# An attention and gated-convolution kernel: stages by a schedule table, and the carried state added on VectorE

## The chip, the cores and the metric

One core of one Trainium2 chip (trn2). Times are device microseconds (us) of one launch of the whole kernel. A run is called *slow* when it is over 1.5% above the fastest run of the same kernel in the same job; the ratios below use fast runs only. *Span* is the part of the time between the first and the last instruction in the trace, some 2 us less than the time. Engines: PE is TensorE, DVE is VectorE, ACT is ScalarE, POOL is GpSimd; SP issues the transfers.

## The reference, cut

```python
B, H, S, D = 4, 8, 768, 48
for t in range(S):                                    # linear attention with decay
    cur = einsum('bhd,bhe->bhde', u * k[:, :, t], v[:, :, t])
    y[:, :, t] = einsum('bhd,bhde->bhe', r[:, :, t], state + cur)
    state = w[..., None] * state + einsum('bhd,bhe->bhde', k[:, :, t], v[:, :, t])
x = y.transpose(0, 2, 1, 3).reshape(B, S, 384)
gate = sigmoid(causal_conv5(x, conv_w))               # one filter of 5 taps for each channel
out = (gate * (x @ w_val)) @ w_out
```

Both kernels work in chunks of 128 tokens and in units of two chunks: 12 units, three for each batch. Inside a chunk the recurrence is a masked attention; between chunks the state `z` is carried, decayed by `w` to the power 128. Four batches of six chunks need 20 state products, and 16 of them have an earlier state to add.

## The kernel before: what the change touches

The state of a chunk is four products into PSUM, and the carried state is added there by one more product, with the identity:

```python
def state(n, cl):
    # ... four products of ks and vb into kv_ps (cut)
    if c > 0:
        nc.tensor.matmul(
            out=kv_ps.rearrange("p n a d -> p (n a d)"),
            lhsT=ident,
            rhs=st["z"].rearrange("p n a d -> p (n a d)"),
            start=False, stop=True, skip_group_check=True,
        )

def decay(n, cl):
    # ... (cut)
    z = wk.tile([128, NP, 2, D], BF16, name="z", bufs=6)
    nc.vector.tensor_tensor(out=z, in0=st["kv_ps", n, cl], in1=wcm, op=ALU.mult)
```

The order of work is a plain loop, the same on every engine. It works on unit `i` and finishes unit `f = i - 1`; what prepares unit `i + 1` is called in between:

```python
w_bc = consts.tile([128, H, D], F32)
nc.sync.dma_start(out=w_bc, in_=w.partition_broadcast(128))
load_r(0)                       # r of a whole batch, then k and v of unit 0, k of unit 1
load_kv(0, "kv")
load_kv(1, "k")
# ... weights, more k and v (cut)
for i in range(N + 1):
    f = i - 1
    # ... loads of k and v of unit i + 3, of r of a later batch (cut)
    if ok(f):
        y_out(f)
    if ok(i + 1):
        cast_v(i + 1)
        scale_k(i + 1, nc.gpsimd)
    if ok(i):
        attn(i, 0); mask_at(i, 0); bonus(i); state(i, 0); decay(i, 0)
    # ... scaling of r, bonus_v(i), weight casts when i == 0 (cut)
    if ok(f):
        conv(f); value(f)
    if ok(i):
        attn(i, 1); mask_at(i, 1); state(i, 1); decay(i, 1)
    # ... transposes of r and k, prod(i + 1) (cut)
    if ok(f):
        project(f)
```

## Time and profile before

| | before |
|---|---|
| time, median of 3 runs | 119.07 us (118.67 to 119.47) |
| profiled run: span | 115.8 us |
| busy: PE, DVE, ACT, POOL | 86%, 58%, 63%, 57% of the span |
| first y products of unit 0, 3 and 11 start at | 22.95, 48.99, 105.69 us |

The first y products of a unit are the first thing that a round does on PE, so their start times cut the execution into a head (up to unit 3), steady rounds (units 3 to 11) and a tail. This is the busy time by stretch of the kernel before. Columns: stretch and its length in us, then busy us and instruction count of PE, weight loads, DVE, ACT and POOL, then granted PE clock, DMA share and GB/s.

```profile
22.95:48.99 26.04, 24.85 (x506) 18.37 (x505) 15.33 (x24) 18.70 (x31) 24.16 (x20) 0.87 0.99 239
48.99:105.69 56.70, 54.79 (x1272) 40.69 (x1272) 39.75 (x61) 38.35 (x70) 30.72 (x21) 1.00 0.66 161
105.69:115.80 10.11, 4.94 (x121) 3.48 (x120) 1.28 (x3) 3.47 (x8) 0.00 (x0) 0.95 0.23 80
```

The lines show three stages with different limits. In the head POOL is busy 24 of 26 us and the DMA share is 0.99. In the steady stage PE is busy 54.8 of 56.7 us and DVE only 39.8. In the tail no engine is full: it is one chain.

### The profile page before, as it was taken

What the parts mean: (1) busy time and instruction counts of PE and PEld (TensorE: products, weight loads), DVE (VectorE), ACT (ScalarE), POOL (GpSimd) and SP (SyncE); (2) the same over time, 40 slices, a digit from 0 to 9 for tenths busy, and PEclk for the clock granted to TensorE, in tenths of its full rate; (3) what the DMA queues carried; (4) which work ended last, traced back from release to release, by engine and by line L of the source; (5) the groups of instructions that cost most, each with busy time, mean ns of one, the idle gap of its engine ahead of it and who ended that gap; (6) DMA issues with size and microseconds to landing.
All of it is one profiled execution on the core that took longest, in us unless ns stands there. A gap on an engine that the chain in (4) does not pass through costs nothing.

```text
span 115.8 us, 4806 instructions
## 1 busy us (share of the span) xinstructions
PE 100.0 (86%) x2098; PEld 76.5 (66%) x2098; DVE 67.7 (58%) x120; ACT 73.0 (63%) x130; POOL 66.3 (57%) x62
## 2 busy tenths in 40 slices
PE   5999046889899999999979999999999999998840
PEld 5998043666667778768747786786777677775610
DVE  5425327926467737767665677774786877775120
ACT  4198375293388696886862958859667483935430
POOL 7942106799999949989549768190462805050000
PEclk9999975555999999999999999999999999999998
DMA  1899599999998998998999795994984030030303
GB/s 44 240 270 150 95 236 305 194 193 266 277 191 180 292 332 169 256 213 253 341 170 248 154 248 113 256 206 96 238 169 147 0 133 8 24 118 6 136 3 136
DMA packets 58677, 20.57 MB, mean 178 GB/s; under 512 B 50592, under 2 KB 58656, under 8 KB 58656
## 3 DMA queue, kind: packets, MB, share of 16 engines
q1 hardware_dynamic: 58432, 20.26, 73.2%
q8 instruction: 16, 0.26, 1.0%
q0 software_dynamic: 224, 0.01, 0.3%
q14 instruction: 5, 0.04, 0.1%
HBM read 15.54 MB, written 4.72 MB: 175 GB/s over the span
## 4 chain that ended last, share of the span: by engine, by line
PE 55%; ACT 10%; SPq 10%; POOL 10%; issue 6%; DMA 4%; DVE 1%; POOLq 0%; ACTq 0%; DVEq 0%
PE mm_ps L383 9%; PE mm_ps L456 9%; SPq L72 8%; PE mm_ps L426 6%; PE mm_ps L435 6%; PE mm_ps L475 6%; PE at_ps L317 5%; ACT kT L268 4%; DMA k_st<-in_k_dram 4%; PE tr_ps L238 3%; PE kv_ps L343 3%; POOL ks L245 3%; ACT o_sb L482 3%; ACT rT L239 3%; PE mm_ps L291 2%
## 5 line engine op out<-in xcount | busy, mean ns | idle before, releaser
L329 DVE TENSOR_TENSOR at<-at_ps,mask 128x1024 bf16<-128x1024 f32 x24 | 29.3, 1220 | 8.8 <-PE at_ps L317 8.8
L303 POOL TENSOR_TENSOR dv<-v_st,s_sb 128x768 bf16<-128x768 f32 x12 | 17.7, 1475 | 24.3 <-DVE s_sb L300 24.3
L245 POOL TENSOR_TENSOR ks<-k_st,dk 128x768 bf16<-128x768 f32 x11 | 20.0, 1815 | 5.5 <-DMA k_st<-in_k_dram 5.5
L463 DVE TENSOR_TENSOR hT<-mm_ps,gate 128x256 bf16<-128x256 f32 (+1 forms) x24 | 13.4, 558 | 15.3 <-PE mm_ps L456 15.3
L226 POOL TENSOR_TENSOR rs<-r_st,dr 128x576 bf16<-128x576 f32 x12 | 16.7, 1412 | 3.2 <-DMA r_st<-in_r_dram 3.1
L268 ACT COPY kT<-tr_ps 128x1024 bf16<-128x1024 bf16 x12 | 12.2, 1014 | 8.6 <-PE tr_ps L265 8.6
L239 ACT COPY rT<-tr_ps 128x768 bf16<-128x768 bf16 x15 | 11.9, 799 | 7.0 <-PE tr_ps L238 7.0
L475 PE MATMUL mm_ps<-wout,hT 128*128 128x384 bf16 x72 | 14.0, 327 | 1.2 <-DVE hT L463 1.2
L456 PE MATMUL mm_ps<-xT,wval 128*128 128x256 bf16 x108 | 13.8, 272 | 0.0
L254 ACT CAST vb<-v_st 128x768 bf16<-128x768 f32 x12 | 10.0, 836 | 5.2 <-DMA v_st<-in_v_dram 5.2
L482 ACT COPY o_sb<-mm_ps 128x384 f32<-128x384 f32 x24 | 10.7, 495 | 3.9 <-PE mm_ps L475 3.9
L279 DVE TENSOR_TENSOR pr<-tr_ps,rT 128x1024 bf16<-128x1024 bf16 x12 | 8.3, 692 | 7.9 <-ACT kT L268 7.6
L411 ACT CAST xT<-mm_ps 128x384 bf16<-128x384 f32 x24 | 11.8, 496 | 1.0 <-PE mm_ps L383 0.2
L317 PE MATMUL at_ps<-rT,kT 48*128 48x128 bf16 x192 | 10.4, 229 | 1.4 <-DVE rT L239 0.6
L456 PEld LDWEIGHTS <-wval 128*128 128x128 bf16 x108 | 10.6, 98 | 1.5
L368 DVE TENSOR_TENSOR z<-kv_ps,wcm 128x384 bf16<-128x384 f32 x20 | 11.0, 548 | 0.0
L265 PE MATMUL tr_ps<-ident,ks 128*128 128x128 bf16 x96 | 7.8, 227 | 3.3 <-DVE ks L245 3.1
L500 PE MATMUL mm_ps<-ident 128*128 128x128 bf16 x130 | 9.4, 248 | 1.4 <-POOL ident masks.py:199 1.4
L500 PEld LDWEIGHTS <-ident 128*128 128x128 bf16 x130 | 9.3, 114 | 1.4 <-POOL ident masks.py:199 1.4
L383 PE MATMUL mm_ps<-at,vb 128*32 128x128 bf16 x384 | 10.1, 227 | 0.0
L435 PE MATMUL mm_ps<-xT,cwd 128*128 128x256 bf16 x60 | 9.3, 286 | 0.9 <-issue 0.9
L444 ACT ACTIVATE gate<-mm_ps 128x512 bf16<-128x512 f32 x12 | 7.2, 597 | 4.6 <-PE mm_ps L435 4.6
(65 smaller groups left out, 150.5 us busy)
## 6 DMA issues: line engine op xcount, KB each, us to landing
k_st<-in_k_dram SPq DMA_DIRECT2D x24, 192.0 KB, 5.2
v_st<-in_v_dram SPq DMA_DIRECT2D x24, 192.0 KB, 5.2
out_dram<-o_sb SPq DMA_DIRECT2D x11, 384.0 KB, 4.0
r_st<-in_r_dram SPq DMA_DIRECT2D x6, 576.0 KB, 5.9
r_st<-in_r_dram SPq DMA_DIRECT2D x4, 288.0 KB, 5.6
wv_st<-in_moe_w_val_dram SPq DMA_DIRECT2D x1, 576.0 KB, 5.8
wo_st<-in_moe_w_out_dram SPq DMA_DIRECT2D x1, 384.0 KB, 5.4
out_dram<-o_sb SPq DMA_DIRECT2D x2, 192.0 KB, 1.9
```

Of the source, the lines that this page charges most:

```text
L226: eng.tensor_tensor(out=rs_t[p][:, :, :, 0:D].rearrange("p j a d -> p a j d"), in0=r_st[b][:, hs, :].rearrange("p a (j d) -> p a j d", d=D ...
L239: (nc.vector.tensor_copy if dve else nc.scalar.copy)(out=st["rT", b][:, p, :].rearrange("x (p j) -> x p j", j=J), in_=tr.rearrange("x j p ...
L245: eng.tensor_tensor(out=ks_t[n % 3][:, :, :, :, 0:D].rearrange("p c n a d -> p c (n a) d"), in0=k_st[n], in1=dk[:, None, :, :].to_broadcas ...
L268: nc.scalar.copy(out=st["kT", n].rearrange("x n (c i) -> x c n i", c=U), in_=tr)
L303: nc.gpsimd.tensor_tensor(out=dv_t[n % 2].rearrange("p c (h d) -> p (c h) d", d=D), in0=v_st[n].rearrange("p c h d -> p (c h) d"), in1=st[ ...
L317: nc.tensor.matmul(out=at_ps[:, par, p, :], lhsT=kT[rows, p, cs], rhs=rT[rows, p, cs], start=(p == 0), stop=(p == NP - 1), skip_group_chec ...
L329: nc.vector.tensor_tensor(out=st["at", n, cl].rearrange("p a n i -> p (a n) i"), in0=st["at_ps", n, cl].rearrange("p a n i -> p (a n) i"), ...
L383: nc.tensor.matmul(out=y_ps[32 * q : 32 * q + 32, T, :], lhsT=lt, rhs=rh, start=q not in first, stop=last, skip_group_check=True,)
L435: nc.tensor.matmul(out=g02[:, 1, :], lhsT=cwd2[:, t, :], rhs=xT[:, 2, t0 + t : t0 + t + W], start=False, stop=(t == KW - 1), skip_group_ch ...
L456: nc.tensor.matmul(out=v_ps[:, i, :], lhsT=wval[:, kt, ts.start + i, :], rhs=xT[:, kt, t0 : t0 + W], start=(kt == 0), stop=(kt == NT - 1),)
L475: nc.tensor.matmul(out=o_ps, lhsT=hT[:, i, cl * C : cl * C + C], rhs=wout[:, i, :], start=(i == 0), stop=(i == NT - 1),)
L500: nc.tensor.matmul(out=t_, lhsT=ident, rhs=ident, start=True, stop=True)
```

## The change

Its intent, as far as the code tells it: (1) the state is carried by a VectorE addition in place in PSUM, which takes the identity product off PE; (2) a text table, probably worked out with a model of the engines' queues, gives the order of some thirty stages, one item for each stage and half unit, so that what waits on one engine stands between items that don't; (3) loads come in the order of need, in pieces of one unit, and stores only when every load has been issued, with ten output buffers in place of three; (4) the tables that the head needs are smaller (decay of r with 2 columns in place of 6, convolution weights prepared on DVE); (5) masks, gates and gated products are split in halves for this, and the third convolution tile is computed as 64x64 blocks. Cut to its core (the numbers after a colon are unit offset and half; `~7` asks for that many warm-up products):

```diff
-        if c > 0:
-            nc.tensor.matmul(out=kv_ps..., lhsT=ident, rhs=st["z"]..., start=False, stop=True, ...)
+    def carry(n, cl):
+        kv_ps = st["kv_ps", n, cl]
+        nc.vector.tensor_tensor(out=kv_ps, in0=kv_ps, in1=st["zin", n, cl], op=ALU.add)
 ...
-    def load_r(b):                 # 288 or 576 KB of a batch, rows of 1152 B
+    def load_r(n):                 # 384 KB of a unit, rows of 384 B
 ...
-        at_ps = ps_at.tile([128, 2, NP, 128], F32, name="at_ps")
+        at_ps = [ps_at.tile([128, NP, 128], F32, name="at_ps") for par in range(2)]
 ...
-    for i in range(N + 1):
-        f = i - 1
-        ...
+    LOADS = """
+        r0 k0 r2 v0 r1 k1 k2 v1 Wv k3 Wo r3 v2 r4 v3 k4 v4 r5 k5 r6 k6 v5 k7 r7 v6 k8 v7 r8 k9 v8
+        r9 k10 v9 r10 k11 v10 r11 v11
+    """
+    HEAD = """ ... """             # units 0 to 3, item by item, with 30 warm-up products (cut)
+    STEP = """
+        Y:-1.0 YE:-1.0 Y:-1.1 A:0.1 YE:-1.1 M:0.3 A:0.0 RS:1.0 M:0.2 KS:1.0 M:0.0 CV:0.0 C:-1.0
+        S:0.0 M:0.1 RT:1.0 V:-1.0 SE:0.0 SG:-1.0 HT:-1.0 V:-1.1 KV:0.0 SG:-1.1 RE:1.0 HT:-1.1
+        ID:0.0 KT:1.0 KE:1.0 O:-1.1 O:-1.0 OE:-1.1 ZE:0.0 PR:1.0 KV:0.1 ID:0.1 OE:-1.0 ZE:0.1
+        DV:0.0
+    """
+    TAIL = """ ... """             # the end of unit 11 (cut)
+    run(HEAD, 0)
+    for i in range(HEAD_STEPS, N):
+        run(STEP, i)
+    run(TAIL, 0)
```

Here Y is the y products, A attention, M masks, C convolution, V value, O output projection, KV state products, ID the in-place addition, ZE decay, CV the cast of v; an E marks a copy out of PSUM.

## The prediction

> **What bounds the kernel now.** I read the page's busy sums and the 40 slices first, then the chain of work that ended last in order of time, then busy time by stretch, then the groups by form.
>
> ```profile
> PE 100.0 (86%) x2098; PEld 76.5 (66%) x2098; DVE 67.7 (58%) x120; ACT 73.0 (63%) x130; POOL 66.3 (57%) x62
> PE   5999046889899999999979999999999999998840
> ...
> PEclk9999975555999999999999999999999999999998
> DMA  1899599999998998998999795994984030030303
> ```
>
> TensorE (PE) is busy 86% of the span and nearly always after slice 10; the holes are in the first 30 us, where the granted clock is also halved. So there are two stages with different limits: a head up to about 35 us, and a steady part. The DMA row is full until about 80 us, so transfers are a near second bound.
>
> The chain in order of time shows the head:
>
> ```profile
> 13.09 4.30 DMA k_st<-in_k_dram
> ...
> 17.58 1.77 POOL ks L245
> ...
> 20.91 1.47 POOL dv L303
> 22.38 1.22 POOL cwd L198
> ```
>
> The chain runs through the queue that issues loads, the second k tile, then one GpSimd (POOL) instruction after another until 32 us. From 35 us it is PE. One steady round:
>
> ```profile
> 85.96 1.30 PE mm_ps L383 x80
> 87.26 0.33 PE at_ps L317 x8
> 87.59 0.28 PE mm_ps L291 x8
> 87.88 0.19 PE kv_ps L343 x4
> 88.07 0.67 PE mm_ps L426 x20
> 88.74 0.66 PE mm_ps L435 x5
> 89.40 0.98 PE mm_ps L456 x9
> ```
>
> There is no wait between these pieces. The rounds start (first y matmuls, L383) at 41.78 and 105.76 us, nine rounds apart: 63.98/9 = 7.1 us each. Busy time by stretch confirms it:
>
> ```profile
> 72.50:80.00 7.50, 7.49 (x174) 5.74 (x174) 5.03 (x9) 5.71 (x11) 3.25 (x2) 1.00 0.96 213
> 93.00:99.50 6.50, 6.44 (x146) 4.66 (x141) 4.86 (x8) 4.08 (x9) 1.48 (x1) 1.00 0.18 63
> ```
>
> Columns: stretch, length, then busy us of PE, weight loads, VectorE (DVE), ScalarE (ACT), POOL; clock, DMA share, GB/s. PE is full, DVE two thirds busy. Moving work from PE to DVE is the right direction.
>
> **What the Trainium skill says.** (1) "VectorE: DVE Perf Modes", section on the TRN2 errata: an fp32 tensor_tensor takes (N+151)/0.96 ns. The trace agrees, also with one operand in PSUM: 1224, 691 and 557 ns by the formula for N = 1024, 512, 384, against 1220, 692 and 548 measured.
>
> ```profile
> L329 DVE TENSOR_TENSOR at<-at_ps,mask 128x1024 bf16<-128x1024 f32 x24 | 29.3, 1220 | 8.8 <-PE at_ps L317 8.8
> L368 DVE TENSOR_TENSOR z<-kv_ps,wcm 128x384 bf16<-128x384 f32 x20 | 11.0, 548 | 0.0
> L463 DVE TENSOR_TENSOR hT<-mm_ps,gate 128x512 bf16<-128x512 f32 x12 | 8.3, 692 | 3.1 <-PE mm_ps L456 3.1
> L352 PE MATMUL kv_ps<-z,ident 128*128 128x384 bf16 x16 | 5.6, 350 | 0.0
> ```
>
> (2) "TensorE: Matmul & The Clock Gate", Part 1: the array falls to half clock after an idle window of about 3.4 us. The trace agrees: PE does nothing from 11.5 to 14.6 us and the clock is 0.50 from 16 to 30 us. (3) "PSUM — Partial Sum Buffer", on bank collisions: engines must be kept apart by bank, not by address. So with one state buffer the next chunk's state matmuls wait until both the new add and the decay have left the bank; the trace of before has only the decay there. (4) "DMA: Bandwidth & Descriptors", Specifications: below 512 B a transfer is not at line rate. The trace agrees: late stretches that only store rows of 1536 B move 63 GB/s at 0.18 share, 350 GB/s per full share, while the first k and v rows of 192 B move 134 to 164 GB/s at a full share (8 to 11 us).
>
> **The change part by part.**
>
> *PE, per unit of 256 tokens.* Removed: the identity product, 0.16 us in the chain, 16 in all, 4/3 per unit = 0.21 us. The third convolution tile, five 128x128 products (0.66 us), becomes 20 products of 64x64 on 128 columns. The existing 20 of that kind on 256 columns take 0.67 us, so half the columns is about 0.33 us: 0.33 saved. The value product has the same total of columns (9 x 256 = 6 x 256 + 6 x 128): unchanged. Transposes of r are the same 96, now 8 in each unit (0.45 us as for k) and no longer twelve in some rounds; those rounds lost another 0.3 us to ScalarE copies. Sum: 1.30 (y) + 0.66 (attention) + 0.28 (bonus) + 0.47 (state) + 0.67 + 0.33 (convolution) + 0.98 (value) + 0.90 (transposes) + 0.98 (project) = 6.57 us, against 7.1 now.
>
> *DVE, per unit.* Four masks of 512 at 0.69 = 2.77 (was 2 x 1.22 = 2.44); two gated products of 384 at 0.55 = 1.10 (was 0.69 + 0.43 = 1.12); decay 20 x 0.548/12 = 0.91; the new in-place add, 16 x about 0.55/12 = 0.73; bonus product 0.69; its copy 0.16. Sum 6.36 us, was 5.32. So DVE comes within 0.2 us of PE. The split masks buy something for this: the first half can begin when half the scores are there, in four banks in place of one pair.
>
> *ACT, per unit:* two y copies 0.99, k and r copies of 1024 elements 1.01 each, v cast 0.84, two sigmoids of 384 about 0.98, two output copies 0.99: 5.8 us. *POOL:* 1.82 + 1.48 + r scaling of 768 elements (1.41 for 576, so about 1.85): 5.15 us. Neither binds.
>
> *DMA.* Busy time now is 0.732 x 115.8 = 84.8 us per engine. Stores: 3072 rows of 1536 B at 70 ns (21.9 GB/s per engine, from the 63 GB/s at 0.18) / 16 = 13.4 us. That leaves 71 us of loads: r 4.72 MB and the weights and w 1.38 MB at the same rate per byte 13.5 and 3.9 us, so 54 us for the 24 k and v tiles of a unit, 2.25 each. r goes from 1152 B rows to 384 B rows, three times as many; if cost is per byte nothing is added, with a fixed cost per packet my estimate is up to 5 us. Loads: 71 to 76 us, about 6 per unit. Started at about 3 us, the last v lands at 74 to 79 us, and stores are held until every load is issued.
>
> *Head.* The order of loads is by need: one third of the r of a batch, then k, in place of the whole r of a batch and a broadcast w of 192 KB. The decay table has 2 columns in place of 6: two exponentials of 384 elements (0.6 us each) in place of twelve (4.3 us). Convolution weights leave POOL (3.8 us, L198 and L206 at 20 to 26 us) for DVE before the first data. Estimate: decay table ready at 5.7 us, first r scaled at 6.5, k landed at about 8, scaled and copied at about 10, first y products near 13.5 us (22.95 now). Then loads pace it: in the new order nine k and v tiles at 2.25, five of r at 1.4 (1.1 by bytes, 0.3 for the shorter rows) and 3.4 of weights stand up to k of unit 4, 31 us from a start at 3: it lands near 34 us, and the head table needs it at its end. PE work in the head: 3 units x 6.57 + 3.2 for what is prepared of units 3 and 4 = 22.9, plus warm-ups of 3, from 6.5 us: 32. So y of unit 3 starts at about 36 us. Now it starts at 49.3 (chain, the ACT o_sb piece before the y products at 49.82).
>
> *Sum.* Eight more rounds to y of unit 11. The pure PE pace is 6.57; with DVE at 6.36 on the other side of every hand-over I choose 6.8: 36 + 8 x 6.8 = 90.4. Tail: now 105.76 to 115.8 = 10.0 us; less 0.33 of convolution and about 0.7 by interleaving, 9. Span 99.4. The time was 119.07 for a span of 115.8, 3.3 more, though the profiled run itself was 117.56, only 1.8 more. I add 2: **101.5 us**, a gain of 15%: about 13 us from the head, 2 from the eight steady rounds, 1 from the tail.
>
> **The rivals.**
> *DVE becomes the bound.* For: 6.36 of 6.57, and the add lengthens the only serial chain (state matmuls, add, decay, next state matmuls in the same buffer) by 0.55 us twice per unit minus 0.16. Against: that chain is about 2.7 us of a 6.6 us round, and a table ordered in advance can fill around it. If so, rounds of 7.1 as now and no steady gain: 36 + 57 + 9 + 2 = 104, and 107 if the head suffers too.
> *DMA bounds it.* For: a full DMA row now and smaller r rows; a starved stretch such as 12 to 14 us now (share 0.40 and 0.23) may recur. Then v of unit 11 lands near 84, y at 87, end 96 to 98 of span if rounds keep pace, but held stores queue up behind: 100 to 106.
> *All goes nearly as the table plans:* rounds of 6.57 and y of unit 3 at 34: 34 + 52.6 + 8.5 + 2 = 97.
> *The head's gain is lost:* PE idles, the clock halves again, in-order queues wait on each other by a wrong model: first 36 us become 45, 110 us. The warm-up products (70 in all against 130 at once) speak against it.
>
> **Range and chances.** The rivals span 97 to 110; 95 to 108 should hold it. Slower by 2% would need the head gain lost and rounds of over 7.6 us at once. Faster 0.95, within 2% 0.03, slower 0.02.
>
> **What would show it.** Right: no matmul of z by the identity and 16 in-place adds near 0.55 us; DVE busy about 78 us and over 75% of the span; PE work down; y of unit 3 at 34 to 39 us; rounds of 6.6 to 7.0; clock full from about 10 us; stores only in the last third. Wrong: rounds of 7.1 or more with PE waiting for DVE; k or v loads as releasers after 40 us; half clock past 20 us; y of unit 0 after 17 us.

## The result, and the profile after

| | before | after |
|---|---|---|
| time, median of 4 runs | 119.08 us (118.67 to 119.47) | 105.53 us (104.37 to 108.75) |
| fast runs of after | | 104.37 and 105.05 us, spans 102.4 and 103.2 |
| slow runs of after | | 106.02 and 108.75 us; the latter is the profiled one, span 106.9 |
| ratio | | 0.8793 (95%: 0.8724 to 0.8863) |

The ratio is the mean time of one kernel's fast runs over that of the other's of the same rounds, so not quite the ratio of the medians. The change makes the kernel 12% faster in this job; measured again on chip 3 (a0 below) it is 9% (ratio 0.9103, 0.8948 to 0.9258), 106.47 against 117.04 us. The before of this job, 119.08 us, is the slowest of all jobs (fast means of 116.31 to 117.31 us in the others), so some 2 us of its gain may not be the change's. The profile of after is of a slow run, and this has to be kept apart from the rest: fast profiles come from two variants below that cost nothing measurable, the identity variant and the one with long warm-ups.

From the page of the kernel after: the sums, then rows of the 40 slices.

```profile
PE 92.6 (87%) x2263; PEld 74.2 (69%) x2263; DVE 76.4 (71%) x151; ACT 73.1 (68%) x120; POOL 64.4 (60%) x64
PE   4996775899999999899299999998999999999740
PEclk9999999557999999999859999999999999999999
DMA  0999989989988989889699989797979993310404
```

PE does 7.4 us less than before and DVE 8.7 us more. The hole in PE moved from the first quarter to one slice in the middle (a 2), with a dip of the clock behind it. The DMA row is full until about 88 us; its last full slices are the stores, which now wait for the loads.

From the groups of instructions by form (line, engine, operation, tiles, shapes, count; busy us and mean ns; idle before and what ended it):

```profile
L360 DVE TENSOR_TENSOR at<-at_ps,mask 128x512 bf16<-128x512 f32 x48 | 30.3, 682 | 7.4 <-PE at_ps L347 7.3
L387 DVE TENSOR_TENSOR kv_ps<-kv_ps,z 128x384 f32<-128x384 f32 x16 | 8.9, 557 | 1.0 <-PE kv_ps L375 0.9
L500 DVE TENSOR_TENSOR hT<-at_ps,gate 128x384 bf16<-128x384 f32 x24 | 12.8, 555 | 8.5 <-PE at_ps L487 8.2
```

The 16 in-place additions take 557 ns each and wait 1.0 us in all: they are there as forecast and are no bottleneck of their own. (48 masks of 682 ns would be 32.7 us; the row has 30.3 because two masks in a row overlap a little. The same holds for DVE as a whole: the 66 DVE instructions of the last six rounds below last 38 us one by one, and DVE is busy 35 us.)

Busy time by stretch of the kernel after, cut at the same events:

```profile
13.47:40.68 27.21, 24.69 (x571) 19.64 (x571) 20.30 (x38) 18.67 (x28) 20.32 (x15) 0.87 0.94 211
40.68:97.56 56.88, 52.95 (x1427) 42.62 (x1426) 45.82 (x87) 43.17 (x74) 35.03 (x21) 0.97 0.83 200
97.56:106.90 9.34, 4.58 (x158) 3.52 (x158) 1.05 (x2) 3.22 (x7) 0.00 (x0) 1.00 0.24 86
```

Set against before: unit 3 starts 8.31 us earlier, the eight steady rounds take 0.18 us *more* in this profile, and the tail 0.77 us less. 8.31 - 0.18 + 0.77 = 8.90 us, which is the difference of the two spans. The fast runs are another 3.7 to 4.5 us shorter. So two questions stand: where the gain of the head comes from and why it isn't larger; and what the steady rounds lost in the profiled run.

The six last rounds before the tail (units 5 to 11) leave out the hole in the middle. First the kernel before, then after, in the same columns:

```profile
64.33:105.69 41.36, 40.70 (x953) 30.32 (x953) 30.01 (x47) 27.94 (x52) 18.92 (x13) 1.00 0.54 130
```

```profile
57.80:97.56 39.76, 38.39 (x1071) 31.01 (x1070) 34.77 (x67) 31.47 (x55) 24.08 (x15) 1.00 0.78 202
```

A round went from 6.89 to 6.63 us; PE is still nearly full and DVE rose from 73% to 87% of the stretch. One such round of after in the chain that ended last (start, length, piece):

```profile
78.09 1.23 PE mm_ps L405 x80
79.33 0.55 PE at_ps L347 x16
79.88 0.03 issue
79.91 1.02 PE mm_ps L456 x40
80.93 0.29 PE kv_ps L317 x8
...
83.29 1.09 PE at_ps L512 x6
84.38 0.17 PE kv_ps L375 x4
84.55 0.45 PE mm_ps L405 x24
```

It is the same picture as the round of before in the prediction: PE work end to end, without the identity product, with 40 convolution products in 1.02 us where there had been 25 in 1.33 us. And this is the hole, in the same view:

```profile
49.77 1.02 PE mm_ps L456 x38
50.78 1.97 issue
52.75 0.32 PE mm_ps L456 x2
```

"issue" means that PE waited for nothing that the profile shows. Two single microseconds of it, by stretch:

```profile
51.00:52.00 1.00, 0.00 (x0) 0.00 (x0) 1.00 (x2) 0.00 (x0) 0.00 (x0) 1.00 0.84 154
53.00:54.00 1.00, 1.00 (x18) 1.00 (x17) 0.17 (x1) 0.87 (x2) 0.27 (x1) 0.50 0.99 195
```

PE stops in the middle of a run of 40 independent convolution products, with nothing to wait for, and 2 us later goes on at half clock until 56 us. The round from unit 4 to 5 took 9.91 us in place of 6.6.

**The pauses sit at fixed instruction numbers.** Counted from the trace, from 0 and in order of start, with weight loads, products and the few semaphore instructions of PE, every PE pause marked "issue" after the first y products that puts over 0.4 us between two starts (25 of them in the 14 traces) begins at a PE instruction whose number leaves 193 when divided by 256 (1985 here; 705, 1473, 2241, 2753, 3009, 3265, 3521 and 3777 in others), whatever the program does there. The trace also has a queue named *instruction*, which moved 17 packets of 16,384 bytes in this kernel, about one for every 256 PE instructions. The long pause ended 1.3 us after such a packet had landed (50.16 to 51.44 us), and all 25 ended 1.0 to 1.6 us after one. The kernel before has one too: 0.90 us at number 1985, at 60.06 us. The Trainium skill, "Runtime: NRT & Kernel Launch", section "Instruction fetch mechanics", says that instructions are refilled in blocks of 16 KiB, 256 instructions, and that crossing a boundary costs a bump of a queue's tail, "mostly hidden". The block size agrees with the packets. "Mostly hidden" holds by number: of 226 crossings after the first y products, 180 put at most 0.15 us between two starts. It does not hold for these 25 pauses.

### The profile page after: what moved, and what is told of

It reads as the page before. It is cut to its first block, busy times and chain, and to the rows that moved or that the text cites. A ratio compares the mean times of both kernels' runs of the same rounds, so it can differ in the third digit from the quotient of the medians.

```text
span 106.9 us, 5141 instructions
## 1 busy us (share of the span) xinstructions
PE 92.6 (87%) x2263; PEld 74.2 (69%) x2263; DVE 76.4 (71%) x151; ACT 73.1 (68%) x120; POOL 64.4 (60%) x64
## 4 chain that ended last, share of the span: by engine, by line
PE 41%; SPq 14%; DVE 11%; issue 9%; DMA 9%; ACT 6%; POOL 5%; DVEq 0%; POOLq 0%
SPq L71 10%; PE mm_ps L405 9%; DMA r_st<-in_r_dram 9%; PE mm_ps L456 8%; PE at_ps L512 5%; PE at_ps L478 4%; PE at_ps L347 4%; PE at_ps L244 4%; DVE hT L500 3%; POOL rs L230 3%; DVE at L360 3%; PE kv_ps L375 2%; DVE z L392 2%; DVE kv_ps L387 2%; ACT o_sb L525 2%
## 5 line engine op out<-in xcount | busy, mean ns | idle before, releaser
L360 DVE TENSOR_TENSOR at<-at_ps,mask 128x512 bf16<-128x512 f32 x48 | 30.3, 682 | 7.4 <-PE at_ps L347 7.3
L230 POOL TENSOR_TENSOR rs<-r_st,dr 128x768 bf16<-128x768 f32 x10 | 18.2, 1822 | 2.8 <-DMA r_st<-in_r_dram 2.8
L500 DVE TENSOR_TENSOR hT<-at_ps,gate 128x384 bf16<-128x384 f32 x24 | 12.8, 555 | 8.5 <-PE at_ps L487 8.2
L252 ACT COPY rT<-at_ps 128x1024 bf16<-128x1024 bf16 (+1 forms) x13 | 15.8, 1228 | 4.0 <-PE at_ps L244 4.0
L456 PE MATMUL mm_ps<-xT,cwd 64*64 64x256 bf16 (+1 forms) x500 | 13.8, 251 | 3.7 <-issue 2.4
L469 ACT ACTIVATE gate<-mm_ps 128x384 bf16<-128x384 f32 x24 | 10.4, 487 | 9.4 <-PE mm_ps L456 9.4
L456 PEld LDWEIGHTS <-cwd 64*64 64x64 bf16 x500 | 12.0, 110 | 5.3 <-issue 3.9
L512 PE MATMUL at_ps<-wout,hT 128*128 128x384 bf16 x72 | 14.7, 327 | 1.0 <-DVE hT L500 0.7
L525 ACT COPY o_sb<-at_ps 128x384 f32<-128x384 f32 x24 | 10.7, 489 | 4.4 <-PE at_ps L512 4.4
L478 PE MATMUL at_ps<-xT,wval 128*128 128x256 bf16 x72 | 12.5, 285 | 0.0
```

The lines of the kernel that those rows point to most:

```text
L230: eng.tensor_tensor(out=rs_t[n % 2][:, :, ps[0] : ps[1], :, 0:D].rearrange("p s n a d -> p (n a) s d"), in0=r_st[n][:, hs], in1=dr[:, hs], ...
L252: nc.scalar.copy(out=st["rT", n][:, ps[0] : ps[1], :].rearrange("x n (i s) -> x s n i", s=2), in_=st["r_tr", n, ps[0]],)
L360: nc.vector.tensor_tensor(out=st["at", n, cl][:, par], in0=st["at_ps", n, cl][par], in1=mask[:, None, :].to_broadcast([128, NP, 128]), op= ...
L456: nc.tensor.matmul(out=g_ps[i][64 * qo : 64 * qo + 64, o0 : o0 + n0], lhsT=cwd[rows, T, t, :], rhs=xT[rows, T, t0 + c0 + t : t0 + c0 + t + ...
L478: nc.tensor.matmul(out=v_ps[:, 0:W], lhsT=wval[:, kt, i, :], rhs=xT[:, kt, t0 : t0 + W], start=(kt == 0), stop=(kt == NT - 1), skip_group_ ...
L500: nc.vector.tensor_tensor(out=st["hT", n][:, i], in0=st["v_ps", n, i], in1=st["gate", n][:, i], op=ALU.mult)
```

## The experiments

Two theories of the steady rounds were set against each other: PE sets their length and the addition on DVE is free, or DVE has become a second bound and the trade gives back what it takes. For the head: the order of the loads sets it, or the decay tables and warm-ups, or the short rows of the loads. For the hole: instruction fetch at a fixed number, or a wait that the profile fails to name. The smaller decay tables and the convolution in 64x64 blocks were not tried alone, nor was the new order of loads in the kernel before.

| label | edit | chip | fast runs, mean us | ratio to before |
|---|---|---|---|---|
| a0_same | none | 3 | 106.47 (2 of 4) | 0.9103 |
| a1_identity | carry by the identity product | 3 | 105.14 (2 of 4) | not given |
| a2_pe_probe | 0.33 us more of PE per round | 3 | 104.94 (2 of 4) | 0.8972 |
| a3_dve_probe | two small DVE operations, inputs in SBUF | 3 | 113.29 (4 of 4) | 0.9687 |
| a3b_dve_probe | two small DVE copies out of PSUM, 0.33 us per round | 8 | 106.89 (3 of 4) | 0.9190 |
| b1_inplace | *before*, with the in-place addition alone | 12 | 114.92 (4 of 4) | 0.9804 |
| a4_plain_order | plain order in the steady table | 12 | 113.29 (4 of 4) | 0.9666 |
| a5_old_loads | loads in the old order | 12 | 113.67 (4 of 4) | 0.9679 |
| a6_long_rows | contiguous loads, wrong result | 12 | 105.14 (4 of 4) | 0.8970 |
| a8_no_warm | no warm-up products | 8 | 105.47 (3 of 4) | 0.9068 |
| a9_stores_early | stores before waiting loads | 8 | 106.87 (2 of 4) | 0.9188 |
| a10_long_warm | 70 warm-ups become 20 long ones | 8 | 105.44 (2 of 4) | 0.9156 |

The fast runs of the kernel before meant 117.04 us on chip 3, 117.31 on 12 and 116.31 on 8. The unedited kernel after was not run on 8 and 12; its own ratio was 0.8793 in the first job and 0.9103 on chip 3, so a difference of 2% between jobs says nothing. For small effects I therefore use the *net round* from the traces: the six rounds from unit 5 to 11, less the gaps between starts at the instruction numbers of the fetch, over six. It is 6.35 to 6.39 us in the five traces whose edits don't touch these rounds' work (after, a0, a6, a8, a10) and 6.39 in a5, so 0.04 us is its noise.

**a0_same: nothing edited.**

> The changed kernel again, unedited, to get a profile in the fast state (the first one fell in the slow state, with TensorE at half clock from 52.6 to 56.0 us after a pause of 1.97 us). Theory P (a slip of the clock made the first profile slow): span 102 to 104 us, clock above 0.97, no round near 9.9 us, rounds of y from unit 5 to unit 11 of 6.6 to 6.8 us, y of unit 3 at about 40.5 us as before. Rival Q (the round of 9.9 us is part of the design): the same long round again.

Measured: 105.68 to 109.54 us, two fast and two slow. The profiled run is slow again (span 107.5), and its hole is at the same place: 2.61 us of "issue" from 50.06 us, at PE instruction 1985, with half clock from 51.8 to 58.6 us; the round from unit 4 to 5 took 11.72 us. Here the clock was full from 14.2 us until the hole, so the hole and the half clock after it make this run slow. The hole belongs to the program and its size varies from run to run.

**a1_identity: the carry back on PE.**

```diff
-        nc.vector.tensor_tensor(out=kv_ps, in0=kv_ps, in1=st["zin", n, cl], op=ALU.add)
+        nc.tensor.matmul(out=kv_ps..., lhsT=ident, rhs=st["zin", n, cl]..., start=False, stop=True, ...)
```

> The state carried by the product with the identity again, all else as changed: TensorE +16 x 0.16 = 2.6 us, VectorE -8.9 us. Theory P (TensorE still sets the rounds, at 6.7 us): rounds longer by 0.21 us, about 8 rounds, +1.5 to +2 us in all. Rival D (VectorE sets the rounds): 2 to 4 us faster. Rival N (the carry buys nothing either way): within 0.7 us.

Measured: 105.14 us for the fast runs against 106.47 for the unedited ones of the same chip, two runs each and overlapping: no difference to be seen. The net round is 6.405 us against 6.37, 0.03 longer, where PE does 0.21 us more and DVE 0.74 us less in each. By stretch, units 3 to 11 of this variant:

```profile
40.01:94.43 54.42, 51.92 (x1436) 42.68 (x1436) 39.83 (x76) 42.89 (x73) 36.30 (x22) 1.00 0.87 213
```

DVE fell to 73% and nothing got faster or slower. In the tuned kernel the addition in place is a swap without profit. It is also the first fast profile of the table: head to 40.01 us, eight rounds in 54.42, tail 9.27, span 103.7 us.

**a2_pe_probe: 0.33 us more PE work in every round.**

```diff
-        ID:0.0 KT:1.0 KE:1.0 O:-1.1 O:-1.0 ...
+        ID:0.0 KT:1.0 KE:1.0 O:-1.1~6 O:-1.0 ...
```

> Six extra 128x128 products of 128 columns, about 0.055 us each, in each of the eight steady rounds: 0.33 us of TensorE work per round, nothing else. Theory P (TensorE bound): +2.6 us. Rival D (VectorE bound): +0 to 1 us.

Measured: net round 6.499 us, 0.13 longer, some 40% of what was added. The time shows nothing (8 x 0.13 = 1 us is within the scatter). PE alone would have given 0.33.

**a3_dve_probe: a probe of DVE that measured something else.**

```diff
+        if n >= 4 and cl == 0:
+            for _ in range(2):
+                nc.vector.tensor_tensor(out=junk, in0=ones16, in1=ones16, op=ALU.mult)   # 128x16, SBUF
```

> Two extra 128x16 fp32 products on VectorE (0.16 us each) in each of the eight steady rounds, into a tile nobody reads: 0.33 us of VectorE work per round. Theory P (TensorE bound, VectorE with slack of some 0.9 us per round): +0 to 1 us. Rival D (VectorE bound): +2.6 us.

Measured: 113.29 us, some 7 us slower than the unedited kernel on the same chip, for 16 tiny operations. The summary of that line in the trace (durations in ns, minimum, median, maximum), then two pieces of the timeline (start, length, piece):

```profile
L398 DVE TENSOR_TENSOR junk<-ones x16: 165/1232/1747, 45.8 to 101.7; 128x16 f32<-128x16 f32 x16
```

```profile
69.52 1.81 POOL L233 TENSOR_TENSOR rs<-r_st,dr 128x768 bf16<-128x768 f32 x1
...
69.92 3.21 DVE L398 TENSOR_TENSOR junk<-ones 128x16 f32<-128x16 f32 x2
...
71.29 1.81 POOL L262 TENSOR_TENSOR ks<-k_st,dk 128x768 bf16<-128x768 f32 x1
```

Each of the twelve operations that met a POOL instruction ended within 0.05 us of the end of one (here 71.36 and 73.13 us, against 71.33 and 73.10 for POOL); the four in the last two rounds, where POOL has no work left, took 165 to 176 ns. This agrees with the Trainium skill, "SBUF — State Buffer", section "Who interferes with whom": a DVE instruction with two SBUF inputs contends with a GpSimd instruction that reads SBUF, and the lock is exclusive. It also shows what the design avoids: in the steady rounds every DVE operation of the changed kernel reads one operand from PSUM, and the in-place addition does so too. As a probe of DVE's load this run is void.

**a3b_dve_probe: the same size, out of PSUM.**

```diff
+        for _ in range(2 if n >= 4 else 0):
+            nc.vector.tensor_copy(junk, st["s_ps", n])
         nc.vector.tensor_copy(st["s", n], st["s_ps", n])
```

> The VectorE probe again, without the fault of the first (two SBUF inputs, 1.01 us each beside GpSimd): two extra copies of the 128x16 bonus sums out of PSUM, 0.165 us each, in each of the eight steady rounds, 0.33 us of VectorE per round. Theory P (TensorE bound, VectorE with slack): +0 to 1 us against the unedited kernel, rounds of units 5 to 11 at most 0.1 us longer than 6.6. Rival D (VectorE bound, or both in turn): rounds longer by 0.2 to 0.33 us.

From its groups by form:

```profile
L331 DVE COPY junk<-kv_ps 128x16 f32<-128x16 f32 x16 | 2.7, 170 | 0.7 <-PE kv_ps L318 0.5
```

Measured: net round 6.557 us, 0.18 longer, some 55% of the 0.34 us added. So neither engine alone sets the round: each probe passes on about half of what it was given. That both set it in turn fits this, but rests on one profile for each probe. The prices hold for the places where the probes stood; they don't add up to the result of a1 (0.74 us of DVE against 0.21 of PE came out even), so where in the order a piece stands counts as much as its length.

**b1_inplace: the in-place addition alone, in the kernel before.**

```diff
-        if c > 0:
-            nc.tensor.matmul(out=kv_ps..., lhsT=ident, rhs=st["z"]..., ...)
 ...
+        if c > 0:
+            kv = st["kv_ps", n, cl]
+            nc.vector.tensor_tensor(out=kv, in0=kv, in1=st["z"], op=ALU.add)
```

> The kernel before with only the carry changed: 16 identity products out of TensorE (0.16 us each), 16 in-place adds of 0.55 us on VectorE. Theory P (TensorE bound, VectorE with slack): at most 2.6 us faster; since the add lengthens the wait for the single state buffer by 0.4 us in each chunk I expect -1 to -2 us. Rival N (the carry alone is worth nothing without the new order, since PE then waits for the add): within 1 us or slower.

Measured: ratio 0.9804 (0.9741 to 0.9868), 2.4 us: faster, though not surely by 2%. Its last six rounds by stretch, to be set against the line of before above, and the new group:

```profile
62.61:102.79 40.18, 39.71 (x946) 29.84 (x945) 34.05 (x55) 27.95 (x52) 20.29 (x14) 1.00 0.59 142
```

```profile
L360 DVE TENSOR_TENSOR kv_ps<-kv_ps,z 128x384 f32<-128x384 f32 x16 | 8.9, 555 | 0.0
```

PE does 1.0 us less in six rounds and the rounds are 1.2 us shorter, 0.2 each, which is what the identity product cost there. From unit 3 to 11 the two profiles differ by 2.35 us, of which 0.6 us is a shorter fetch pause. (b1 also starts unit 0 2.0 us earlier, with a single carry before it, and loses 1.5 of that again by unit 3; so the profiles can't divide the 2.4 us more closely.) Here DVE had a quarter of its time free, and in the steady rounds the trade pays in full.

**a4_plain_order: the table without its order.** The steady items stand in the order of the old loop; everything else is as in after.

```diff
-        Y:-1.0 YE:-1.0 Y:-1.1 A:0.1 YE:-1.1 M:0.3 A:0.0 RS:1.0 M:0.2 KS:1.0 M:0.0 CV:0.0 C:-1.0
-        S:0.0 M:0.1 RT:1.0 V:-1.0 SE:0.0 SG:-1.0 HT:-1.0 V:-1.1 KV:0.0 ...
+        Y:-1.0 YE:-1.0 Y:-1.1 YE:-1.1 CV:0.0 KS:1.0 A:0.0 M:0.0 M:0.1 S:0.0 SE:0.0 KV:0.0 ID:0.0
+        ZE:0.0 RS:1.0 DV:0.0 C:-1.0 SG:-1.0 SG:-1.1 V:-1.0 HT:-1.0 V:-1.1 HT:-1.1 A:0.1 ...
```

> The steady rounds in the plain order of the kernel before (same stages, same buffers, same head and tail tables), so only the order in the table for units 4 to 11 is undone. Theory S (the tuned order is what keeps TensorE fed with VectorE nearly full): rounds of 7.1 to 7.5 in place of 6.7, +3 to +6 us. Rival L (TensorE's shorter work alone sets the pace, order does little): within 1.5 us.

Measured: 113.29 us, net round 7.76 us, 1.39 longer. From the list of waits in its last six rounds (engine and line waited for; us in all, times, longest), then the chain of one round:

```profile
PE kv_ps L375 <- ACT vb L268: 7.0, 6, 1.2
```

```profile
72.04 0.90 ACT xT L437 x2
72.94 0.73 ACT vb L268
...
73.72 0.33 PE kv_ps L375 x4
```

PE waits 1.2 us in every round for the cast of v, which stands on ACT behind the copies of y. A second wait ends within 0.1 us of it: the weight loads of the same products wait for the copy of the bonus sums, which ends at 73.57 us on DVE behind two masks (the cast ends at 73.66). So moving the cast alone would have gained little. In the tuned table the state products come after convolution, bonus, transposes and value, 2.8 us of PE work that fills the time of the cast. The wait before the state products is most of the 1.39 us. It says what the order is worth among the table's other choices, not against the old loop, whose net round is 6.88 us: there the cast was called a unit ahead.

**a5_old_loads: the loads in the old order.**

```diff
-        r0 k0 r2 v0 r1 k1 k2 v1 Wv k3 Wo r3 v2 ...
+        r0 r1 r2 k0 v0 k1 Wv Wo v1 k2 v2 r3 r4 r5 k3 v3 ...
```

> The loads in the order of the kernel before (all r of a batch first, weights before the second v), head table unchanged. Theory H (the head's gain comes from what is loaded first): k of unit 0 lands about 3 us later, v of units 1 and 2 later too, y of unit 3 at 44 to 47 us in place of 40.5, +4 to +6 us in all. Rival W (the head is bound by its work, not by what has landed): under +2 us.

Measured: 113.67 us. Unit 0 starts at 15.90 us, but unit 3 only at 49.59, where after has 40.68 and before 48.99; the net round is unchanged (6.387). From its waits between 14 and 50 us:

```profile
POOL ks L259 <- DMA k_st<-in_k_dram: 8.5, 2, 5.2
...
PE tr_ps L283 <- POOL ks L259: 4.8, 2, 4.6
```

So in this kernel the order of the loads is worth 8.9 us of the head, as much as the whole head gained (8.31): k of units 1 and 2 had been standing behind r of the whole batch and the weights. The rest of the change does bring the first product forward by 7 us (22.95 to 15.90), and all of that is lost again while POOL waits for k. (What the order of loads would bring the old loop, without the smaller tables and the new order of work, was not tried.)

**a6_long_rows: are the short rows of the loads the next limit?** k, v and r are read as contiguous rows of 1536 and 3072 B, which is the wrong data (relative error 1.41).

> Wrong result on purpose: k, v and r are loaded as contiguous rows of 1536 or 3072 bytes per partition in place of 192 and 384, same bytes, same instructions otherwise. Theory H (the head waits for loads): y of unit 3 from 40.5 to 34 to 37 us, total -4 to -7 us. Rival W (the head is bound by its work): within 1.5 us.

Measured: 105.14 us, ratio 0.8970. Its head by stretch:

```profile
13.63:41.31 27.68, 24.41 (x571) 19.72 (x571) 21.75 (x38) 18.69 (x28) 20.95 (x16) 0.90 0.99 347
```

347 GB/s in place of 211, with a mean clock of 0.90 against 0.87, and unit 3 starts no earlier: 41.31 us against 40.68. Counted by packets in the order of issue, k of unit 4 had landed by 22.2 us here and by 33.7 us in after. In the new order the speed of the loads doesn't set the head. (Half clock for some 5.5 us of this stretch could hide 2 to 3 us at most, as it could in the profile of after. In one fast profile, a1, the chain that ended last does pass through a landing of k, at 24.12 us; a6 has no such wait left on POOL and gains nothing.)

**a8_no_warm: no warm-up products at all.** `spin` and `warm` return at once.

> No warm-up products at all. Theory C (the head needs the full clock): half clock from the start to 20 us or beyond, y of unit 3 at 42 to 44 us in place of 40, +1.5 to +4 us. Rival W (the head waits for other engines' hand-overs, the clock matters little there): within 1 us. By theory F the long pause at instruction 1985 should also move, to 140 instructions later in the program.

Measured: 105.47 us. The clock was half until 15.6 us and from 19.0 to 25.9 us in the profile, and unit 3 still started at 40.44. The long pause did not move to a later place, as the expectation had it: nothing is left at number 1985, and smaller pauses are at 1473 (0.45 us), 2241 (0.26) and 3265 (0.68). Not distinguishable from the unedited kernel; the warm-ups buy nothing that these runs can show.

**a9_stores_early: a store goes out as soon as its unit is done,** even while loads are held back for a buffer.

> Outputs stored as soon as they are ready in place of after the last load is issued. Theory L (loads have slack once the head is over): within 1 us. Rival S (holding the stores back is what keeps loads in time): stores wait in the issuing queue for the output copies and hold up the loads behind them, rounds of 7 us or more, +2 to +4 us.

Measured: 106.87 us for two fast runs (106.19 and 107.55). The net round is 6.554, 0.18 longer. The rounds speak for holding the stores back, the times leave it unclear.

**a10_long_warm: move the place of the fetch.** The 70 warm-ups of 128 columns become 20 of 384 or 512, which takes 100 PE instructions out (the expectation says 19 and 102; the trace shows 20, and 4426 instructions in place of 4526) before the steady rounds, so that instruction 1985 falls into another round.

> The 70 warm-up products of 128 columns become 19 of 512 or 384 columns: about the same TensorE time, 102 TensorE instructions fewer before the steady rounds. All unexplained pauses of TensorE so far begin at its instruction number 193 modulo 256 and end 1.0 to 1.6 us after a 16384-byte packet of the instruction queue has landed. Theory F (TensorE runs out of fetched instructions when a densely issued stretch meets a late packet): the long pause at instruction 1985, now in the convolution of unit 4 after the densest stretch, moves to the start of the y products of unit 5, after the sparsest one, and shrinks below 0.5 us or goes; the clock stays full there; 102 to 104 us, with no run above 105. Rival C (the pause belongs to that place in the program or to that time): it stays in the convolution at about 50 us, 104 to 109 us as before.

Measured: the hole left the convolution of unit 4, and the round from unit 4 to 5 took 6.28 us. Pauses appeared at 705 (1.46 us), 2241 (0.51) and 3009 (0.72). The one at 2241, in the chain:

```profile
55.66 0.96 PE mm_ps L459 x34
56.62 0.51 issue
57.13 0.30 PE mm_ps L459 x6
```

So the place follows the instruction number and not the program, as the fetch theory has it; a missed wait would have stayed with the convolution of unit 4. a4 fits too: its rounds, in which PE idles 1.4 us longer, have no pause at any of these numbers. But the time did not improve (105.08 to 108.84 us, two slow runs of four): the pauses moved and did not go. Why the fetch at 1985 is so often the late one stays open.

No variant clearly beats the kernel after.

## Why the prediction was right, and where its steps failed

The time, 105.53 us, lies in the range of 95 to 108; the forecast gain of 17.6 us was 13.5, and 10.6 us on chip 3. Its sum, term by term, against the profiled slow run and the fast profile of a10:

| term | predicted | after (slow) | a10 (fast) |
|---|---|---|---|
| y of unit 0 starts | 13.5 | 13.47 | 13.47 |
| y of unit 3 starts | 36 | 40.68 | 40.29 |
| eight rounds | 54.4 | 56.88 | 53.72 |
| tail | 9 | 9.34 | 9.3 |
| outside the span | 2 | 1.85 | 1.8 |

**The start was right.** The first y products came within 0.03 us of the step-by-step estimate. Two of its steps were off, in opposite directions: the decay table was ready at 6.5 us in place of 5.7, and k of unit 0 had landed by 6.6 in place of 8.

**The step that failed is "Then loads pace it", with the PE work beside it at 32 us.** The landing itself was forecast well (k of unit 4 near 34 us; 33.7 in after), but it is not what the end of the head waits for: loads don't pace the head in the new order, as a6 shows at a like clock, and they do with the old order of loads (a5). The estimate of PE was the nearer thought but assumed an engine that never waits: it set 25.9 us of work after 6.5 us. In a10 at full clock PE was busy 28.3 us (5.56 up to 13.47 us and 22.76 up to 40.29) and idle 5.5 us. 6.5 + 28.3 + 5.5 = 40.3. So of the 8 us between 32 and 40, about 2.4 are work that I undercounted and 5.5 are standstill: 1.46 in one fetch pause, the rest in hand-overs of 0.9 us and less, before attention (ACT's copy of k), key transposes (POOL's scaling), the first state products (ACT's cast of v) and the bonus products (DVE). The 4.3 us of this term, less 0.7 by which the rounds came out shorter, are the 3.6 us by which a10's profiled run (105.08) exceeds 101.5. (The start of unit 3 in before was also misread: 49.3 is near the second half of its y products; the first began at 48.99. So the head gained 8.3 us in after and 8.7 in a10, where about 13 were forecast.)

**The rounds were right in size, and the reason was half right.** Eight rounds at 6.8 were 54.4 us, against 53.72 in a10 and 54.42 in a1. "Pure PE pace 6.57" was near as well: the net round is 6.37. That DVE at 6.36 on the other side of every hand-over would lengthen it is what the two probes show, each at about half price. But the gain of the swap itself, 0.21 us per round on PE, was counted in full, and a1 shows that in this kernel it brings 0.03.

**DVE as the bound** did not come about: 76.4 us busy was forecast as 78, but 71% of the span where "over 75%" was set as the mark. The 6.36 us per unit were right as a sum of durations (38.1 us in six rounds), but DVE was busy only 5.8 us a round, as its instructions overlap, and so stayed 0.6 us below PE's 6.4, not 0.2. **DMA as the bound** neither: the r rows of 384 B cost more, as allowed for. Counted from the trace, the packets of r took 305 us of engine time in place of 248, 3.6 us for each of 16 engines, inside the "up to 5". The last v landed at some 80 us, later than the 74 to 79 forecast but 14 us or more before y of unit 11 (97.56, and 94.01 in a10). What the prediction takes from its third skill point, PSUM banks, no run here tests.

**The clock was wrong.** "Full from about 10 us" failed in the profiled run (half from 18.5 to 25.3 us) and held in a1 and a10. It may have cost about 1 us: the profiles in which the clock dips between 18 and 27 us start unit 3 at 40.31 to 41.31 us (after, a2, a3b, a6, a8), the others at 38.93 to 40.29 (a0, a1, a3, a4, a9, a10; a5, with the old loads, left out). Whether the dip causes the delay or comes from the same waits isn't shown.

**What no step had: the fetch pauses.** In the profiled run 1.97 us of standstill and 3.4 us at half clock made one round 9.91 us. The three slow profiles (after, a0, a2) have pauses of 1.97, 2.61 and 1.73 us at instruction 1985, the fast ones with the tuned table 1.2 us at most at that number. In after the long round accounts for 3.3 of the 3.7 to 4.5 us by which its span exceeds the fast ones. So the pauses explain the slow profiles of after and a0 and go with that of a2; for slow runs without a profile it is only likely.

**Where the gain lies, then.** About 8 us come from the head, and they go when the old order of loads is put back (a5). The net steady round went from 6.88 to 6.37 us, 0.5 each, of which the in-place addition gives nothing now, though it is worth about 2% to the kernel before (b1); how the rest divides between the cheaper convolution and the order was not tried apart. The tail gives 0.8.

## What to carry to other kernels

Taken from this one case: before shaving the busiest engine, look at what stands in front of what in the load queue: the same loads in order of need were worth more than all the rest here. A trade between engines is worth its full price only while the receiver has free time. Once both are near 90% busy, price it by a probe on each side and by swapping it back, and give a VectorE probe an operand in PSUM while GpSimd works.

## What the Trainium skill lacked or had wrong

- "Runtime: NRT & Kernel Launch", section "Instruction fetch mechanics": crossing a block of 256 instructions is called mostly hidden, and no size is given for a crossing that isn't. Here 25 of 226 crossings put over 0.4 us between two starts on PE, the longest with 2.61 us of standstill; during the two longest pauses (1.97 and 2.61 us) the clock also fell to half, for 3.4 and 6.8 us.
- "TensorE: Matmul & The Clock Gate", Part 1: it names an idle window of about 3.4 us before the clock falls. Here the clock fell during single pauses of 1.97 and 2.61 us, and not at one of 1.73 us. In all 14 traces every change of clock lies a whole multiple of 3.41 us after the first one, and the half-clock stretches were 3.4, 6.8 or 13.7 us long. In the 3.41 us before those two falls PE was idle 1.87 and 1.72 us, while the 1.73 us pause lay across such a step. No threshold comes out of this: other falls had as little as 0.93 us of idle before them.
- "DMA: Bandwidth & Descriptors", Specifications: it gives the threshold of 512 B, and neither it nor the rest of the page a measured duration of a packet of these sizes. From the traces a packet of 192 B took 16.3 ns on its engine, of 384 B 24.8 ns and of 1152 B 60.6 ns, so rows of 384 B cost 1.23 times as much per byte as rows of 1152 B.
